# The last step of a top-k attention with a feed-forward layer behind it, and what follows it: exponentials, turns and dense pieces in another order

## The chip, the cores and the metric

The kernel runs on one core of one Trainium2 chip. The metric is the device time of one execution in microseconds (us); lower is better. Of the kernel before there are three runs without a profile and one execution with one.

## The reference

There are 8 batches of 8 heads, 576 tokens and 64 features. For each head the scores are scaled products of queries and keys; in each row only those that reach the 32nd largest are kept, a softmax is taken over them, and the result weighs the values. The heads side by side make 4608 tokens of 512 features, which go through a layer of width 2048 with a squared relu.

```python
scores = scale * np.matmul(q, k.transpose(0, 1, 3, 2))
kth = np.partition(scores, -32, axis=-1)[..., -32:-31]
scores = np.where(scores >= kth, scores, -1e9)
attn = np.exp(scores - np.max(scores, axis=-1, keepdims=True))
attn = attn / (np.sum(attn, axis=-1, keepdims=True) + 1e-09)
x = np.matmul(attn, v)          # then heads side by side: 4608 x 512
h = np.maximum(x @ w_in, 0.0)
out = h * h @ w_out
```

## The kernel before, in words

**Steps.** The attention is cut into U = 144 steps. A step holds 128 query rows of two heads (x = 0 and 1), each with 576 scores. The loop `for u in range(U)` (L688) writes out, by hand, the order in which each engine gets its instructions; `pin` keeps that order. The last four steps, U-4 to U-1, are the last 128 rows of the four head pairs of the last batch, so only when all four are placed is the last block of 128 tokens complete.

**What a step goes through.** `scores` makes the scores on PE (TensorE), and ACT (ScalarE) copies them to `s`. `topk` finds the 32nd largest on DVE (VectorE) by four rounds of MAX8 and three of MATCH_REPLACE8. For most steps `drop` (L373) then computes on POOL (GpSimd), from the negated ends `neg` (L361), what pushes the scores below the bound far down, and a DMA adds it to `s` (L382); `exps` (L386) takes the exponentials on ACT into `w_two`, one of three buffers a, b, c by u % 3; `turn` (L395) transposes `w_two` to `wT` with a DMA on SP's queue. For the last step, and for x = 1 of the one before it (`by_vector`, L355), it goes another way: `early_exps` (L364) takes the exponentials `e` of the unmasked scores on ACT, and `mask` (L388) multiplies them on DVE by the comparison with the bound.

**Turns.** The last two steps are turned by PE: `turn_by_tensor` (L399) makes four transposes for x = 0 and five for x = 1 into a PSUM bank (`sc_a` for U-2, `sc_b` for U-1) and copies each group to `wT`, by ACT for U-2 (L409), by DVE for U-1 (L411). The second group waits for the copy of the first.

**Products and placing.** `weigh` (L413; `products` calls it for both x) multiplies `wT` with the values into `av_ps`, or into `sc_a` for the last two steps, with the sum of the weights as a 65th column: ten matmuls a step. `invert` (L434) takes the reciprocal on DVE, and `place` (L444) scales on ACT into `x_tok`, two instructions a step. In the loop, step U-5 is placed in step U-1, which makes the last block but one complete.

**Blocks.** A complete block of 128 tokens is queued by `turn_x` (L683). For the last blocks of the last batch `x_unit` (L473) puts an entry into `moves`: four transposes of `x_tok` on PE (L489) and a copy `xT` on ACT (L490). Then `block` (L516) adds four *up pieces* to `ups` and, with the last of these, four *down pieces* to `downs`. An up piece is 16 matmuls with `w_in` (L533) into a bank `gen` (two of them) or, for every third once `tail` is set, `sc_b`; behind it come a relu on ACT (L538) and a square, on ACT (L544) or, once `late` is set, on DVE (L542). A down piece is 4 matmuls of 512 columns with `w_out` (L556) into the one bank `dn_ps`; the fourth is followed by a copy on ACT (L561) and a store on SP's queue (L563).

**Dense pieces as filling.** `piece` (L577) runs one piece, taken in turns from `ups` and `downs`. With `later` set it puts the relu and square of an up piece by in the list `behind`; no call before the change sets it. `dense` (L589) runs, for x = 1, one entry of `moves`, and one or two pieces. In the loop, `dense(u, 0)` and `dense(u, 1)` stand near the end of each step. In the last step they stand ahead of `early_exps(u)` and `exps(u - 1, 0)`.

**Behind the loop** (L735 to L771): the three masks, the turns of U-2, the last products, reciprocals and placings, with dense pieces between them; a reduction over flags on DVE (L753), its sum by a matmul (`count`, L761) and a copy (`bad`, L763), which says whether the general path below must run (it doesn't for this input); then the four ups and downs of the last block, each up piece beside a down piece of the block before, and four down pieces at the end.

**Order on the engines before**, from the loop's last step on, as built:

- PE: the products of U-5, two down pieces of the block that stands first, x_tok transposes, an up piece, the products of U-4, the turn of U-2 (sc_a), half the turn of U-1 (sc_b), a down piece, an up piece, the products of U-3, the other half of the turn of U-1, the products of U-2, an up piece, the products of U-1, an up piece, x_tok transposes, a down piece, the count, and then up and down pieces in turns.
- ACT: neg, x_tok (U-5), two exps of U-3 (w_two_a), xT, a relu, a square, neg, two e of U-1, an exp of U-2 (w_two_b), two copies of the turn of U-2, x_tok (U-4), and then relus, squares and x_tok.
- DVE: the last MAX8, three masks, a reciprocal, the first copy of the turn of U-1, a reciprocal, the second copy, two reciprocals, the reduction, and four squares as multiplications.

Of the kernel before, what the change touches and what calls it, by code (L numbers as in the profile page):

```python
# [23 lines left out]
def kernel(  # L24
# [20 lines left out]
    def pin(ins):  # L45
        tc.keep_in_program_order(ins)
        return ins
# [193 lines left out]
    U = len(steps)  # L241
# [113 lines left out]
    def by_vector(u, x):  # L355
        return u == U - 1 or (u == U - 2 and x == 1)

    def negate(u, ends):
        neg = small.tile([128, 2, 2], f32, name="neg", bufs=4)
        got = st[u]["ends"] if ends == 2 else st[u]["ends"][:, :, 0:1]  # L360
        pin(nc.scalar.activation(neg[:, :, 0:ends], got, AF.Copy, scale=-1.0))  # L361
        return neg

    def early_exps(u):  # L364
        d = st[u]
        neg = negate(u, 1)
        d["e"] = {}
        for x in range(2):
            if by_vector(u, x):
                e = d["e"][x] = scp.tile([128, S], bf16, name="e", bufs=3)  # L370
                pin(nc.scalar.activation(e[:, :], d["s"][:, x, :], AF.Exp, bias=neg[:, x, 0:1]))
# [12 lines left out]
    def exps(u, x):  # L384
        d = st[u]
        pin(nc.scalar.activation(w_two[u % 3][:, x, 0:S], d["s"][:, x, :], AF.Exp, bias=d["neg"][:, x, 0:1]))  # L386

    def mask(u, x):  # L388
        d = st[u]
        pin(nc.vector.scalar_tensor_tensor(out=w_two[u % 3][:, x, 0:S], in0=d["s"][:, x, :], scalar=d["m"][3][:, x, 7:8],  # L390
                                           in1=d["e"][x][:, :], op0=ALU.is_ge, op1=ALU.mult))
# [7 lines left out]
    def turn_by_tensor(u, x, by_scalar):  # L399
        if x == 0:  # L400
            st[u]["wT"] = scp.tile([128, 9, 128], bf16, name="wT", bufs=3)
            st[u]["tp"] = ps_sc.tile([128, 2, 1024], bf16, name="sc_" + "ab"[u - U + 2])
        flat = w_two[u % 3][:, :, :].rearrange("p x n -> p (x n)")
        tp = st[u]["tp"][:, x, 0:512 + 128 * x].rearrange("p (n r) -> p n r", r=128)
        for n in range(4 + x):
            pin(nc.tensor.transpose(tp[:, n, :], flat[:, (4 * x + n) * 128:(4 * x + n + 1) * 128], id_h[:, :]))
        to = st[u]["wT"][:, 4 * x:4 + 5 * x, :]
        if by_scalar:
            pin(nc.scalar.activation(to, tp, AF.Copy))  # L409
        else:  # L410
            pin(nc.vector.tensor_copy(to, tp))  # L411
# [15 lines left out]
    def sums(u):  # L427
        if u < U - 2:
            return av
        if not last_two:  # L430
            last_two["ps"] = ps_sc.tile([128, 2, 512], f32, name="sc_a")
        return last_two["ps"][:, u - (U - 2), 0:130].rearrange("p (x d) -> p x d", x=2)

    def invert(u):  # L434
        r = small.tile([128, 2, 1], f32, name="rsum", bufs=4)
        pin(nc.vector.reciprocal(r[:, :, :], sums(u)[:, :, 64:65]))  # L436
        st[u]["r"] = r
# [6 lines left out]
    def place(u):  # L444
        for x, (i, c, a) in enumerate(steps[u]):
            b, pr = pairs[i]
            o, r = sums(u)[:, x, :], st[u]["r"]
            if c < 4:
                if (b, c) not in x_tok:
                    x_tok[b, c] = ffp.tile([128, 512], bf16, name="x_tok", bufs=8)  # L450
                h = 2 * pr + a
                pin(nc.scalar.activation(x_tok[b, c][:, h * 64:(h + 1) * 64], o[:, 0:64], AF.Copy, scale=r[:, x, :]))
                left[b, c] = left.get((b, c), 8) - 1
                if left[b, c] == 0:
                    full.append((b, c))
            else:
                for g in range(2):
                    h, rows = 2 * pr + g, slice(64 * g, 64 * g + 64)
                    pin(nc.scalar.activation(x_rem[b % 2][rows, h * 64:(h + 1) * 64], o[rows, 0:64], AF.Copy, scale=r[rows, x, :]))
                left[b, 4] = left.get((b, 4), 4) - 1  # L460
                if left[b, 4] == 0:
                    soon_moves.append(lambda b=b: rem_unit(b))
        del st[u]


    moves, ups, downs = [], [], []
    soon_moves = []
    ripe = {}
    late, tail = [], []
# [99 lines left out]
    def idle_piece():  # L569
        hp = ps_one.tile([128, 512], f32, name="dn_ps")  # L570
        for kh in range(KH):
            pin(nc.tensor.matmul(out=hp[:, :], lhsT=id_h[:, :], rhs=fill[:, :], start=(kh == 0), stop=(kh == KH - 1)))

    turn_of = [0]
    behind = []

    def piece(later=False):  # L577
        turn_of[0] ^= 1
        for q_ in ((ups, downs), (downs, ups))[turn_of[0]]:
            if q_:  # L580
                rest = q_.pop(0)()
                if rest and later:
                    behind.append(rest)
                elif rest:
                    rest()
                return True
        return False

    def dense(u, x, later=False):  # L589
        for go in ripe.pop(u, ()):  # L590
            go()
        if moves and x == 1:
            rest = moves.pop(0)()
            if rest and later:
                behind.append(rest)
            elif rest:
                rest()
        if x == 1:
            moves.extend(soon_moves)
            soon_moves.clear()  # L600
        N = 2 if (u >= U - 26 and x == 0) or len(ups) + len(downs) > 24 else 1
        for n in range(N):
            if not piece(later and N == 1) and n == 0 and u < U:
                idle_piece()
# [65 lines left out]
    def ok(w):  # L670
        return 0 <= w < U

    def finish(w):
        if ok(w):
            invert(w)
            place(w)

    def products(w):
        if ok(w):
            for x in range(2):  # L680
                weigh(w, x)

    def turn_x(u):  # L683
        for b, c in full:
            x_unit(u, b, c)
        full.clear()

    for u in range(U):  # L688
        for x in range(2):
            if ok(u - 1) and not by_vector(u - 1, x):  # L690
                drop(u - 1, x)
        quads_of(u)
        topk(u, (0,))
        if ok(u - 4):
            invert(u - 4)
        if ok(u + 1):
            for i, c, a in steps[u + 1]:
                while coming <= i or (coming == i + 1 and soon):
                    prepare(u)
            scores(u + 1)  # L700
            both(u + 1)
        casts_next = bool(soon) and soon[0].__name__ == "values"
        for _ in range(0 if casts_next else 2 if u < 8 else 1):
            prepare(u)
        if ok(u - 4):
            place(u - 4)
        if ok(u - 2):
            exps(u - 2, 0)
            exps(u - 2, 1)
            turn(u - 2)  # L710
        fetch(10 if u < 8 else 3)
        if u >= Z:
            turn_x(u)
        topk(u, (1, 2))
        if ok(u + 1):
            pairs_of(u + 1)
            copy_far(u + 1)
            lesser(u + 1)
        topk(u, (3,))
        if casts_next:  # L720
            prepare(u)
        if by_vector(u, 1) and u < U - 1:
            early_exps(u)
        dense(u, 0)
        dense(u, 1)
        if u == U - 1:
            early_exps(u)
            exps(u - 1, 0)
        products(u - 3)
        turn_x(u)  # L730
        if w_casts and u >= 3:
            w_casts.pop(0)()
        if w_loads and u >= 1:
            w_loads.pop(0)()
    mask(U - 2, 1)  # L735
    mask(U - 1, 0)
    mask(U - 1, 1)
    turn_by_tensor(U - 2, 0, True)
    turn_by_tensor(U - 2, 1, True)
    finish(U - 4)  # L740
    turn_x(U)
    turn_by_tensor(U - 1, 0, False)
    dense(U, 0)
    products(U - 3)
    finish(U - 3)
    turn_by_tensor(U - 1, 1, False)
    products(U - 2)
    turn_x(U)
    dense(U, 1)
    products(U - 1)  # L750
    finish(U - 2)
    finish(U - 1)
    pin(nc.vector.tensor_reduce(worst[:, :], flags[:, :, :].rearrange("p f n -> p (f n)"), axis=mybir.AxisListType.X, op=ALU.max))  # L753
    pin(nc.vector.tensor_scalar(worst[:, :], worst[:, :], scalar1=0.0, scalar2=None, op0=ALU.is_gt))
    dense(U, 1)
    turn_x(U)
    late.append(True)
    tail.append(0)
    dense(U + 1, 1)
    count = ps_one.tile([128, 512], f32, name="gen", bufs=2)  # L760
    pin(nc.tensor.matmul(out=count[0:1, 0:1], lhsT=worst[:, :], rhs=ones[:, :], start=True, stop=True))  # L761
    bad = const.tile([1, 1], mybir.dt.int32, name="bad")
# [135 lines left out]
```

## Time and profile before

| | us |
|---|---|
| median of three runs | 940.19 |
| lowest, highest | 939.16, 942.92 |
| the profiled execution | 941.0 |
| its span, first to last instruction | 939.2 |
| DVE busy in it | 895.6 |
| ACT busy in it | 785.8 |
| POOL busy in it | 776.0 |
| PE busy in it | 685.7 |

The profile is of one execution. Engines are PE, PEld (PE's weight loads), DVE, ACT, POOL and SP. A timeline row gives the start in us from the span's start, the duration in us, the engine, the line of the kernel, the operation, the tile written and the tiles read, the shapes, and a count when several in a row are merged; in brackets stands how long the engine was idle before it and what released it. In merged rows of PE the ends are modelled, so the distance from one row's start to the next is the better price of a piece. A windows row gives a stretch, its length, the busy time of PE, PEld, DVE, ACT and POOL in it with the number of instructions, the clock that PE was granted as a share of full speed, the busy share of the DMA engines, and GB/s.

### The profile page before, as it was taken

The numbers are of one execution on the slowest core, as the hardware profiler recorded it, in microseconds if no ns is written. First come the engines' busy times: TensorE is split into PE (matmuls) and PEld (weight loads), VectorE is DVE, ScalarE is ACT, GpSimd is POOL, SyncE is SP. The second block draws the span as 40 slices with busy tenths as digits, with TensorE's granted clock in tenths as the row PEclk, the third lists the DMA queues.
The fourth block names the chain that finished last, engine by engine and source line by source line (L and its number), as shares of the span: only waits on it lengthen the run. The fifth ranks groups of instructions, "written<-read, shape, count | busy, mean of one in ns | idle before, by whom it ended". The sixth has DMA issues, their size and how long they took to land.

```text
span 939.2 us, 20939 instructions
## 1 busy us (share of the span) xinstructions
PE 685.7 (73%) x6176; PEld 434.4 (46%) x6176; DVE 895.6 (95%) x3633; ACT 785.8 (84%) x1780; POOL 776.0 (83%) x803
## 2 busy tenths in 40 slices
PE   6777676777777677776777777767777788787767
PEld 3333344444445444444454444444445455555444
DVE  6999999999999999999999999999999999999972
ACT  4677898889888988889888998888888888987884
POOL 7888889888888888888878889888898887897760
PEclk9998999899999999999989999999998998998989
DMA  5668866899998999889999999999999998886751
GB/s 140 135 156 167 176 133 131 180 196 200 200 199 182 200 205 202 188 191 194 203 189 179 191 207 200 207 184 194 189 205 193 199 211 175 167 180 135 147 115 38
DMA packets 329976, 166.29 MB, mean 177 GB/s; under 512 B 306560, under 2 KB 306560, under 8 KB 329856
## 3 DMA queue, kind: packets, MB, share of 16 engines
q1 hardware_dynamic: 311088, 92.62, 51.9%
q0 software_dynamic: 17568, 71.97, 33.8%
q8 instruction: 52, 0.85, 0.4%
q14 instruction: 68, 0.56, 0.2%
q10 hardware_dynamic: 1200, 0.30, 0.1%
HBM read 37.75 MB, written 9.44 MB: 50 GB/s over the span
## 4 chain that ended last, share of the span: by engine, by line
DVE 65%; issue 11%; ACT 9%; DMA 5%; PE 5%; POOL 2%; SPq 1%; POOLq 0%; ACTq 0%
DVE m L342 27%; DVE cat L346 17%; DVE sc_b L282 6%; DVE cat L292 5%; DVE cat L291 5%; DVE most L283 5%; DMA s<-gone_a 2%; PE sc_b L263 2%; ACT s L266 1%; ACT w_two_a L386 1%; DMA s<-gone_b 1%; PE gen L533 1%; PE dn_ps L556 1%; DVE rsum L436 1%; ACT rl L538 1%
## 5 line engine op out<-in xcount | busy, mean ns | idle before, releaser
L342 DVE MAX8 m<-cat 128x8 f32<-128x104 f32 (+3 forms) x1152 | 448.6, 433 | 0.0
L346 DVE MATCH_REPLACE8 cat<-m,cat 128x104 f32<-128x104 f32 (+2 forms) x864 | 272.1, 324 | 0.0
L307 POOL TENSOR_TENSOR cat<-s 128x576 int32<-128x576 int32 (+1 forms) x144 | 230.5, 1601 | 2.0 <-ACT s L266 2.0
L316 POOL TENSOR_TENSOR cat<-cat,most 128x576 int32<-128x576 int32 (+1 forms) x144 | 190.1, 1320 | 26.7 <-ACT most L298 14.9
L263 PE MATMUL sc_b<-qkT 64*128 64x288 f32 x512 | 109.8, 504 | 124.9 <-DVE cat L292 123.0
L533 PEld LDWEIGHTS <-w_in 128*128 128x128 bf16 x2304 | 152.4, 104 | 48.5 <-issue 27.8
L556 PE MATMUL dn_ps<-w_out,h 128*128 128x512 bf16 x576 | 165.2, 418 | 2.3 <-ACT wide L561 1.5
L533 PE MATMUL gen<-xT,w_in 128*128 128x128 bf16 x2032 | 145.3, 229 | 11.4 <-ACT xT L490 4.6
L266 ACT ACTIVATE s<-sc_b 128x576 f32<-128x576 f32 x144 | 93.3, 648 | 69.5 <-PE sc_b L263 64.4
L378 POOL TENSOR_SCALAR gone_b<-s,neg 128x576 uint8<-128x576 f32 x142 | 105.9, 746 | 30.4 <-ACT neg L361 21.1
L378 POOL TENSOR_SCALAR gone_a<-s,neg 128x576 uint8<-128x576 f32 x143 | 106.6, 746 | 28.2 <-ACT neg L361 18.6
L263 PE MATMUL sc_a<-qkT 64*128 64x288 f32 x512 | 100.6, 468 | 39.3 <-DVE most L283 28.9
L263 PEld LDWEIGHTS sc_b<-qkT 64*128 64x128 f32 x512 | 47.2, 206 | 176.2 <-issue 96.1
L266 ACT ACTIVATE s<-sc_a 128x576 f32<-128x576 f32 x144 | 91.3, 634 | 13.4 <-PE sc_a L263 12.4
L538 ACT ACTIVATE rl<-gen 128x512 f32<-128x512 f32 x143 | 85.7, 599 | 8.1 <-PE gen L533 7.2
L544 ACT ACTIVATE h<-rl 128x512 bf16<-128x512 f32 x140 | 88.2, 630 | 4.4
L422 PEld LDWEIGHTS <-wT 128*128 128x128 bf16 (+1 forms) x1600 | 59.7, 102 | 59.6 <-DMA wT<-w_two_a 24.7
L556 PEld LDWEIGHTS <-h 128*128 128x128 bf16 x576 | 54.6, 104 | 67.3 <-issue 30.7
L386 ACT ACTIVATE w_two_a<-s,neg 128x576 bf16<-128x576 f32 x96 | 69.3, 777 | 5.3 <-DMA s<-gone_a 4.3
L386 ACT ACTIVATE w_two_b<-s,neg 128x576 bf16<-128x576 f32 x95 | 68.7, 779 | 5.5 <-DMA s<-gone_b 3.9
L282 DVE TENSOR_TENSOR sc_b<-sc_a,s 128x288 f32<-128x288 f32 x144 | 66.3, 460 | 5.1 <-ACT s L266 5.0
L382 POOL DMA_DIRECT2D s<-gone_b x61 | 54.1, 888 | 20.2 <-DVE m L342 8.3
(165 smaller groups left out, 1198.4 us busy)
## 6 DMA issues: line engine op xcount, KB each, us to landing
s<-gone_a POOLq DMA_DIRECT2D x61, 576.0 KB, 4.9
s<-gone_b POOLq DMA_DIRECT2D x61, 576.0 KB, 4.7
v_raw<-in_v_dram SPq DMA_DIRECT2D x64, 128.0 KB, 3.2
out_dram<-wide SPq DMA_DIRECT2D x32, 256.0 KB, 4.2
k_raw<-in_k_dram SPq DMA_DIRECT2D x63, 128.0 KB, 3.3
q_raw<-in_q_dram SPq DMA_DIRECT2D x63, 128.0 KB, 3.2
wide<-in_moe_w_in_dram SPq DMA_DIRECT2D x8, 512.0 KB, 4.4
wide<-in_moe_w_out_dram SPq DMA_DIRECT2D x8, 512.0 KB, 4.0
```

Source lines behind the costliest of these rows:

```text
L263: pin(nc.tensor.matmul(out=ps[j][:, x, 0:HALF], lhsT=lhsT, rhs=rhs, start=True, stop=True))
L266: pin(nc.scalar.activation(s[:, :, j * HALF:(j + 1) * HALF], ps[j][:, :, 0:HALF], AF.Copy))
L282: pin(tt(far, one[:, :, QUAR:HALF], two[:, :, QUAR:HALF], op=ALU.max))
L307: pin(tt(less, s[:, :, 0:wide].bitcast(i32), s[:, :, HALF:HALF + wide].bitcast(i32), op=ALU.add))
L316: pin(tt(less, less, d["most"][:, 0:n_h, :, :].bitcast(i32).rearrange("p h x n -> p x h n"), op=ALU.subtract))
L342: pin(nc.vector.max(out=m[r][:, x, :], in_=part(r, x)))
L346: pin(nc.vector.match_replace(out=part(r, x), in_to_replace=m[r][:, x, :], in_values=part(r, x), imm_value=NEG))
L378: pin(nc.gpsimd.tensor_scalar(byte[:, x, :, 1], s[:, x, :], scalar1=d["neg"][:, x, 1:2], scalar2=-HUGE, op0=ALU.add, op1=ALU.mult))
L386: pin(nc.scalar.activation(w_two[u % 3][:, x, 0:S], d["s"][:, x, :], AF.Exp, bias=d["neg"][:, x, 0:1]))
L533: pin(nc.tensor.matmul(out=hp[:, n * n_rows:(n + 1) * n_rows], lhsT=w_in[:, kh, (f0 + n) * 128:(f0 + n + 1) * 128], rhs=xt(kh), start=(kh ...
L538: pin(nc.scalar.activation(rl[:, :], hp, AF.Relu))
L556: pin(nc.tensor.matmul(out=op[:, :], lhsT=held["h2"][:, f, c * 128:(c + 1) * 128], rhs=w_out[:, f, :], start=(f == 0), stop=(f == NF - 1)))
```

## The change

All of it lies in the last step of the loop and behind the loop.

1. In the last step, as soon as U-5 is placed, the complete block is queued and its x_tok transposes and xT copy are made at once, ahead of the exponentials of U-3.
2. `early_exps` of the last step and the exponential of U-2 come ahead of the dense pieces, and there are two pieces instead of three, with their relu and square put by. A third such piece stands between the masks and the turn.
3. The four halves of the two turns follow each other with no dense piece between; behind them come the products of U-2, U-3 and U-1, and the three reciprocals.
4. `late` is set there, so that all squares of the two blocks left are DVE's. Then the relus that were put by run (`flush`), then the three placings.
5. A down piece, the x_tok transposes of the last block, the reduction over the flags, an up and a down piece follow, then the count and the rest as before.

As built, the number of instructions changes on ACT only by the four squares that go to DVE. The order from the last step on is now:

- PE: the products of U-5, x_tok transposes, an up piece, a down piece, the products of U-4, an up piece, the whole turn of U-2, the whole turn of U-1, the products of U-2, U-3 and U-1, a down piece, x_tok transposes, an up piece, a down piece, the count, an up piece, and then down and up pieces in turns, with four down pieces at the end.
- ACT: neg, x_tok (U-5), xT, two exps of U-3 (w_two_a), neg, two e of U-1, an exp of U-2 (w_two_b), two copies of the turn of U-2, x_tok (U-4), two relus, x_tok (U-2, U-3, U-1), xT, and then relus and evictions.
- DVE: the last MAX8, three masks, a reciprocal, both copies of the turn of U-1, three reciprocals, two multiplications, the reduction, and six multiplications.

```diff
             place(u - 4)
+        if u == U - 1:
+            turn_x(u)
+            while moves:
+                moves.pop(0)()
         if ok(u - 2):
...
-        if by_vector(u, 1) and u < U - 1:
+        if by_vector(u, 1):
             early_exps(u)
-        dense(u, 0)
-        dense(u, 1)
-        if u == U - 1:
-            early_exps(u)
+        if u < U - 1:
+            dense(u, 0)
+            dense(u, 1)
+        else:
             exps(u - 1, 0)
+            piece(True)
+            piece(True)
         products(u - 3)
...
     mask(U - 1, 1)
+    def flush():
+        while behind:
+            behind.pop(0)()
+
+    assert not ripe and not moves and not soon_moves
+    piece(True)
     turn_by_tensor(U - 2, 0, True)
     turn_by_tensor(U - 2, 1, True)
     finish(U - 4)
-    turn_x(U)
     turn_by_tensor(U - 1, 0, False)
-    dense(U, 0)
-    products(U - 3)
-    finish(U - 3)
     turn_by_tensor(U - 1, 1, False)
     products(U - 2)
-    turn_x(U)
-    dense(U, 1)
+    products(U - 3)
     products(U - 1)
-    finish(U - 2)
-    finish(U - 1)
+    for w in (U - 2, U - 3, U - 1):
+        invert(w)
+    late.append(True)
+    flush()
+    for w in (U - 2, U - 3, U - 1):
+        place(w)
+    tail.append(0)
+    piece()
+    turn_x(U)
     pin(nc.vector.tensor_reduce(worst[:, :], flags ...))
     pin(nc.vector.tensor_scalar(worst[:, :], worst[:, :], ...))
-    dense(U, 1)
-    turn_x(U)
-    late.append(True)
-    tail.append(0)
-    dense(U + 1, 1)
+    while moves:
+        moves.pop(0)()
+    piece()
+    piece()
     count = ps_one.tile([128, 512], f32, name="gen", bufs=2)
```

More of the change, by code (lines that the diff above doesn't have):

```diff
@@ L740 @@
     finish(U - 4)
-    turn_x(U)
     turn_by_tensor(U - 1, 0, False)
-    dense(U, 0)
-    products(U - 3)
-    finish(U - 3)
     turn_by_tensor(U - 1, 1, False)
     products(U - 2)
+    products(U - 3)
+    products(U - 1)
+    for w in (U - 2, U - 3, U - 1):
[6 more added lines that the diff above has]
+    piece()
     turn_x(U)
-    dense(U, 1)
-    products(U - 1)
-    finish(U - 2)
-    finish(U - 1)
     pin(nc.vector.tensor_reduce(worst[:, :], flags[:, :, :].rearrange("p f n -> p (f n)"), axis=mybir.AxisListType.X, op=ALU.max))
     pin(nc.vector.tensor_scalar(worst[:, :], worst[:, :], scalar1=0.0, scalar2=None, op0=ALU.is_gt))
-    dense(U, 1)
-    turn_x(U)
-    late.append(True)
-    tail.append(0)
-    dense(U + 1, 1)
+    while moves:
+        moves.pop(0)()
+    piece()
+    piece()
     count = ps_one.tile([128, 512], f32, name="gen", bufs=2)
```

## The prediction

> **What bounds the kernel now.** I read the page's busy shares first, then the chain that ended last, then the timeline engine by engine from 899 us on, then the windows.
>
> ```profile
> span 939.2 us, 20939 instructions
> ```
>
> DVE has the highest share and sets the pace: in the windows below it is busy 3.42 of 3.42 us and 3.41 of 3.41 up to 907.17, and it has no gap until its last MAX8. The change leaves every DVE instruction up to there alone. So 906.20 + 1.41 = 907.5 us stays, and the change can only act on the 31.7 us behind it.
>
> ```profile
> 906.20 1.41 DVE L342 MAX8 m<-cat 128x8 f32<-128x576 f32 x2
> 911.08 1.54 DVE L390 SCALAR_TENSOR_TENSOR w_two_c<-s,m,e 128x576 bf16<-128x576 f32 x2 [2.75 <-ACT e L371]
> ...
> 904.34 0.50 ACT L452 ACTIVATE x_tok<-av_ps,rsum 128x64 bf16<-128x64 f32 x2
> 905.09 1.44 ACT L386 ACTIVATE w_two_a<-s,neg 128x576 bf16<-128x576 f32 x2 [0.26 <-DMA s<-gone_b]
> 906.43 0.57 ACT L490 ACTIVATE xT<-gen 128x512 bf16<-128x512 bf16 x1
> ...
> 909.51 0.63 ACT L544 ACTIVATE h<-rl 128x512 bf16<-128x512 f32 x1
> 910.05 0.19 ACT L361 ACTIVATE neg<-m 128x2 f32<-128x2 f32 x1
> 910.27 1.44 ACT L371 ACTIVATE e<-s,neg 128x576 bf16<-128x576 f32 x2
> 911.62 0.76 ACT L386 ACTIVATE w_two_b<-s,neg 128x576 bf16<-128x576 f32 x1
> ```
>
> At 907.5 the selection is done, but the last step's exponentials (e, L371) stand on ACT behind a relu and a square, which wait for a matmul piece. So the masks (L390) sit 2.75 us, and the turn of step U-2 starts only behind w_two_b, at 912.4. From there PE does everything:
>
> ```profile
> 907.06 1.79 PE L533 MATMUL gen<-xT,w_in 128*128 128x128 bf16 x16 [1.94 <-ACT xT L490]
> 908.64 0.76 PE L422 MATMUL av_ps<-vau_e,wT 128*128 128x65 bf16 x10
> 912.43 0.61 PE L406 MATMUL sc_a<-id_h,w_two_b 128*128 128x128 bf16 x4 [3.03 <-ACT w_two_b L386]
> 913.73 0.69 PE L406 MATMUL sc_a<-id_h,w_two_b 128*128 128x128 bf16 x5 [0.69 <-ACT wT L409]
> 914.64 1.91 PE L556 MATMUL dn_ps<-w_out,h 128*128 128x512 bf16 x4
> 916.35 1.57 PE L533 MATMUL gen<-xT,w_in 128*128 128x128 bf16 x16
> ...
> 918.06 0.45 PE L406 MATMUL sc_b<-id_h,w_two_c 128*128 128x128 bf16 x5
> 918.34 0.47 PE L422 MATMUL sc_a<-vau_a,wT 128*128 128x65 bf16 x10
> ...
> 922.22 0.23 PE L489 MATMUL gen<-id_h,x_tok 128*128 128x128 bf16 x1 [0.53 <-ACT x_tok L452]
> 922.28 1.03 PE L556 MATMUL dn_ps<-w_out,h 128*128 128x512 bf16 x4
> ...
> 923.85 1.05 PE L533 MATMUL gen<-xT,w_in 128*128 128x128 bf16 x16 [0.42 <-ACT bad L763]
> 924.74 1.03 PE L556 MATMUL dn_ps<-w_out,h 128*128 128x512 bf16 x4
> 925.60 1.06 PE L533 MATMUL gen<-xT,w_in 128*128 128x128 bf16 x16
> ...
> 930.01 3.62 PE L556 MATMUL dn_ps<-w_out,h 128*128 128x512 bf16 x16
> ```
>
> From start to start, an up piece (L533 x16) takes 0.89 us and a down piece (L556 x4) 0.86 at full clock; PE ends at 930.01 + 3.62 = 933.63. Early in this stretch the same pieces take twice that. The windows, cut every 3.41 us, show why:
>
> ```profile
> 900.34:903.76 3.42, 2.05 (x18) 0.90 (x18) 3.42 (x13) 3.33 (x8) 3.34 (x3) 1.00 0.77 205
> 903.76:907.17 3.41, 1.02 (x9) 0.49 (x8) 3.41 (x16) 2.99 (x7) 2.42 (x3) 1.00 0.60 111
> 907.17:910.58 3.41, 2.23 (x26) 2.06 (x24) 1.16 (x2) 1.63 (x4) 1.45 (x3) 0.50 0.45 87
> 910.58:914.00 3.42, 0.88 (x8) 0.72 (x8) 1.63 (x3) 2.39 (x4) 0.00 (x0) 0.50 0.00 0
> 914.00:917.41 3.41, 3.41 (x22) 2.29 (x21) 0.42 (x1) 1.71 (x4) 0.00 (x0) 0.50 0.00 0
> 917.41:920.82 3.41, 3.41 (x77) 3.41 (x75) 0.83 (x3) 2.68 (x6) 0.00 (x0) 1.00 0.36 82
> ...
> 163.06:166.48 3.42, 3.01 (x29) 2.61 (x29) 3.42 (x11) 3.04 (x8) 2.95 (x5) 0.50 0.80 171
> 166.48:169.89 3.41, 3.19 (x11) 1.07 (x10) 3.41 (x19) 3.17 (x9) 3.16 (x4) 0.50 1.08 264
> ```
>
> The second number is PE's busy time, the third from the end its clock. The clock is 1.00 or 0.50 for a whole window and changes at the edges only. A warm window with 2.05 us busy is followed by a warm one, one with 1.02 by a cold one; of the cold ones, 3.01 is followed by a cold one and 3.41 by a warm one. So the line down lies between 1.02 and 2.05, the line up between 3.01 and 3.41. PE is cold from 907.17 to 917.41: just where the turns stand.
>
> **The change part by part.**
>
> *Early exponentials.* The x_tok transposes now come right behind place(U-5): x_tok ends at 904.84, the last transpose (0.23) at 905.15, and the xT copy (0.5 before the next can start) stands ahead of w_two_a, which starts at 905.7 instead of 905.09: 0.6 later. Behind it, by the rows' starts: w_two_a 1.34, neg 0.2, e 1.35, w_two_b 0.76 end at 909.4 instead of 912.4. Gone from between are the wait for the up piece (907.06 to 908.85), its relu and its square. The masks follow e (908.7) at 0.77 us each and end by 910.3 instead of 912.6. The DMA that turns w_two_a starts 0.6 later on SP; its reader, the products of U-3, comes near 914, so this costs nothing; without that cover 0.6.
>
> *Dense pieces of the last step.* Ahead of the turn PE now has an up piece, a down piece, the products of U-4 and a second up piece, all behind the xT copy, from 905.8. Two down pieces leave the place where they kept PE busy; one now follows the first up piece, the other goes past the turns, and so does the one at 914.64:
>
> ```profile
> 901.36 1.03 PE L556 MATMUL dn_ps<-w_out,h 128*128 128x512 bf16 x4
> 903.24 1.04 PE L556 MATMUL dn_ps<-w_out,h 128*128 128x512 bf16 x4 [0.85 <-ACT h L544]
> ```
>
> Window 900.34 to 903.76 loses 1.03 + 0.52 of its 2.05 us and gains three transposes of at most 0.4, which leaves 0.9: PE goes cold at 903.76, a window earlier. Cold, an up piece takes 1.7 (908.64 - 907.06, of which 0.11 was warm), a down piece 1.7 (916.35 - 914.64), ten products 0.6 to 0.76. So up 905.8 to 907.5, down to 909.2, products to 909.8, and the second up piece would end at 911.5. But window 907.17 to 910.58 is now full, PE is warm from 910.58, and the piece ends at 911.1. The turn starts there, 1.7 us after its data but 1.3 before the turn of before.
>
> *Turns without dense pieces.* Warm, from 911.1: four transposes 0.43, copy 0.66 with its hand-over, five transposes (0.28 until the next starts), four of U-1 0.43, DVE's copy 0.48, five 0.48, and the second copy:
>
> ```profile
> 914.88 0.42 DVE L411 COPY wT<-sc_b 128x512 bf16<-128x512 bf16 x1 [2.17 <-PE sc_b L406]
> 918.54 0.49 DVE L411 COPY wT<-sc_b 128x640 bf16<-128x640 bf16 x1
> ...
> 921.53 1.33 DVE L753 TENSOR_REDUCE worst<-flags 128x1 f32<-128x1152 f32 x1
> 925.57 0.69 DVE L542 TENSOR_TENSOR h<-rl 128x512 bf16<-128x512 f32 x1 [2.52 <-ACT rl L538]
> ...
> 921.64 0.52 ACT L452 ACTIVATE x_tok<-sc_a,rsum 128x64 bf16<-128x64 f32 x2 [0.24 <-DVE rsum L436]
> 922.05 0.60 ACT L538 ACTIVATE rl<-gen 128x512 f32<-128x512 f32 x1
> ```
>
> That is 914.4 (before: 919.0). Products of U-2 and U-3 lie in the wait for it; those of U-1 end at 914.9. Window 910.58 to 914.00 holds about 2.3 us of work (0.5 of the up piece, its 0.15 us drain, 1.15 and 0.5 of turns and products), above the 2.05 of the row that stayed warm: PE stays warm. With drains counted otherwise it is 1.9 to 2.6, so this is close, and its other side is rival B.
>
> *Relus put by.* The two relus (0.60 each) run on ACT behind the U-2 copy, from 913.8 to 915.0, before the reciprocals of the products exist, so they cost nothing; without that cover 1.2. Their squares become DVE multiplications of 0.69 behind the reciprocals, 915.3 to 916.6; PE reads the first at 919.3.
>
> *Placing.* Reciprocals from 914.9, the first result at 915.1; three pairs of x_tok on ACT, 0.42 + 0.42 + 0.50: 916.45; the last transpose starts at 916.5 instead of 922.22. One down piece fills PE meanwhile.
>
> *What is left for PE.* Here the change gives back. Before, four ups and eight downs stood behind that transpose, from 922.28 on; now six ups and nine downs do, 6 x 0.89 + 9 x 0.86 = 13.1, with the count 0.1, and 0.17 for the last matmul's drain. From 916.5 that ends at 929.9. PE is the bound here: the last xT copy is done at 917.3 and its reader comes at 920.1; the flag for the count (1.33 and a short second instruction on DVE, behind the two multiplications) is ready at about 918.0, and PE asks for it at 918.3. Should it be late, PE waits as long.
>
> *Sum.* 933.63 - 929.9 = 3.7 us. Behind PE's end nothing changes: the eviction, the store and the end, 5.6 us. The span becomes 935.5; the profiled execution, 941.0 us, becomes 937.3. It was 0.8 above the median of 940.19, so the median's version is 936.5; I forecast 936.9, between the two.
>
> *Two rules against rows.* Whether the turn counts as work for the clock, and what a gap costs, decides more than any instruction. The window 914.00 to 917.41 began with 0.64 us of transposes and ended in full clock, while a window with 3.01 us busy did not: without the transposes it had 2.77. The Trainium skill, TensorE: Matmul & The Clock Gate, Part 4 (PE-mode transpose), says that transposes do not count as PE work for the gate. By that rule window 910.58 to 914.00 would count about 1.0 us, and the clock would go as in rival B. Window 903.76 to 907.17 had 1.02 us of work and still cost the clock. The same page's Part 1 says that the clock drops after at least one idle window, and no window here would be wholly idle; by that rule PE stays warm, which is rival A, and the row speaks against it.
>
> **The rivals.**
>
> *A. PE is warm as the turn starts.* The edges can lie elsewhere against the work in another execution. If they fall 1.7 to 2.7 us later, which is a third of their 3.41 us, the window that ends near 909 is full, the second up piece runs at full clock and the turn starts at 910.2, 0.9 earlier: 936.4. If PE never goes cold, the turn starts with its data at 909.4, all later steps move up 1.7, and the gain is 5.4: 935.6, or 934.8 against the median. Against it: the 0.9 us of work in the window up to 903.76, less than in the 1.02 row.
>
> *B. PE goes cold in the turn.* If transposes don't count, 914.00 to 917.41 runs at half clock, where PE has about 3 us of work: 1.5 us lost, 938.8; a further half window lost gives 939.6. The warm-up row above speaks against it.
>
> *C. PE doesn't warm before the last block (slower than before).* The place is window 907.17 to 910.58. By the 3.01 row it warms PE only with a hole of less than 0.4 us in it; a late wT of U-4 or a late xT decides. Past that point the second up piece ends at 911.8, the turn goes at half clock as in the rows of before, its waits leave holes in the next two windows as well, and the last transpose stands 6.6 us on (5.6 as worked out, 1.0 for slower transposes and products), at 918.4. Then window 917.41 to 920.82 has a hole too, and PE is cold to 924.24. Of its 13.2 us of work it does 2.9 by then, and ends at 934.7: 1.1 slower, 942.1. Against it: the pieces ahead of the turn wait for nothing but xT and a wT that was issued a step earlier.
>
> *D. Nothing comes of it*, because the tail hangs on stores or code loading: 941. PE's unbroken rows from 923.85 to 933.63 speak against it.
>
> **How the numbers follow.** Forecast (a gain of 2.9 to 4.7): 0.55. A: 0.25. B: 0.10. C: 0.05. D: 0.05. About 0.5%, 4.7 us, is what a measurement of this kernel can tell from no change; the forecast's 3.7 lies below that, A's 5.4 above. Faster by over 0.5%: most of A and a little of the forecast, where the median's scatter carries it over, 0.27; slower by as much: C and a late flag together, 0.04; within: 0.69. The range takes in A against the median (934.8, less 0.4 for the median's own scatter) and B with the further half window (939.6): 934.4 to 939.6. It leaves out C, D and the edges of A and B.
>
> **What would show it.** Right: w_two_b ends near 909.4; the masks follow without the 2.75 us wait; the turn begins at 911 with transposes of full-clock length; the last x_tok transpose stands near 916.5; PE runs from there without a gap for 13.3 us. Wrong: cold windows between 911 and 917 (B, C), PE idle behind 916.5 for the count or for relus, or a turn that starts before 910 (A).

## The result, and the profile after

The changed kernel takes 938.74 us (median of 22 runs, 935.01 to 942.98), the kernel before, run beside it, 942.02 (22 runs, 938.59 to 948.4). The ratio is 0.9966, with a 95% interval of 0.9952 to 0.9980: 3.2 us faster, 1.9 to 4.5. The prediction's 936.9 against 940.19 is 0.9965. In absolute terms 938.74 lies 1.8 above the forecast and inside its range, 934.4 to 939.6; the kernel before stands 1.8 above its first median of 940.19 as well.

The two profiled executions have spans of 939.2 and 936.5 us. But they don't reach the change at the same time: the first mask (L390, right behind the last MAX8) starts at 907.53 before and at 908.90 after, though no instruction up to the last step was moved. In the profiles below that point lies between 902.12 and 917.39. So I measure from there. Two rows of the windows view follow, first before and then after, from the first mask to PE's end; the second number is PE's busy time, the third from the end its mean clock:

```profile
907.53:933.63 26.10, 20.98 (x225) 15.01 (x222) 8.02 (x16) 14.14 (x30) 1.45 (x3) 0.81 0.14 34
```

```profile
908.90:930.87 21.97, 20.14 (x223) 13.22 (x220) 10.57 (x20) 11.34 (x25) 2.35 (x3) 0.96 0.17 40
```

I call this length the *tail*: 26.10 us before, 21.97 after, 4.13 less, at a mean clock of 0.96 instead of 0.81. Each tail, here and below, is that of one execution. Behind PE's end both need 5.6 us for the last eviction and store. The timeline of after, DVE, ACT and then PE:

```profile
907.57 1.43 DVE L342 MAX8 m<-cat 128x8 f32<-128x576 f32 x2
908.90 0.82 DVE L390 SCALAR_TENSOR_TENSOR w_two_b<-s,m,e 128x576 bf16<-128x576 f32 x1
909.62 1.78 DVE L390 SCALAR_TENSOR_TENSOR w_two_c<-s,m,e 128x576 bf16<-128x576 f32 x2
...
914.54 0.49 DVE L411 COPY wT<-sc_b 128x640 bf16<-128x640 bf16 x1 [0.53 <-PE sc_b L406]
...
907.12 1.43 ACT L386 ACTIVATE w_two_a<-s,neg 128x576 bf16<-128x576 f32 x2
908.45 0.19 ACT L361 ACTIVATE neg<-m 128x2 f32<-128x2 f32 x1
908.68 1.44 ACT L371 ACTIVATE e<-s,neg 128x576 bf16<-128x576 f32 x2
910.02 0.76 ACT L386 ACTIVATE w_two_b<-s,neg 128x576 bf16<-128x576 f32 x1
...
914.36 1.10 ACT L538 ACTIVATE rl<-gen 128x512 f32<-128x512 f32 x2
915.88 0.52 ACT L452 ACTIVATE x_tok<-sc_a,rsum 128x64 bf16<-128x64 f32 x2 [0.43 <-DVE rsum L436]
...
907.27 1.86 PE L533 MATMUL gen<-xT,w_in 128*128 128x128 bf16 x16 [0.69 <-ACT xT L490]
908.93 1.85 PE L556 MATMUL dn_ps<-w_out,h 128*128 128x512 bf16 x4
910.62 0.47 PE L422 MATMUL av_ps<-vau_e,wT 128*128 128x65 bf16 x10
910.92 1.06 PE L533 MATMUL gen<-xT,w_in 128*128 128x128 bf16 x16
911.82 0.39 PE L406 MATMUL sc_a<-id_h,w_two_b 128*128 128x128 bf16 x4
912.89 0.44 PE L406 MATMUL sc_a<-id_h,w_two_b 128*128 128x128 bf16 x5 [0.69 <-ACT wT L409]
...
914.95 0.50 PE L422 MATMUL sc_a<-vau_b,wT 128*128 128x65 bf16 x10
...
927.25 3.62 PE L556 MATMUL dn_ps<-w_out,h 128*128 128x512 bf16 x16
```

The masks no longer wait: the 2.75 us that stood behind e is gone. w_two_b ends at 910.78, 1.88 behind the first mask (before: 4.85). The turn starts at 911.82, at 2.92 (before: 4.90), right behind the second up piece, and its transposes have the length of the full clock (0.39 instead of 0.61). The two relus that were put by run in a row at 914.36, ahead of the first x_tok, which waits for the reciprocals anyway. The windows of after, cut at the same edges as those of before, which happen to fit this execution too:

```profile
900.34:903.76 3.42, 2.06 (x27) 1.23 (x25) 3.42 (x11) 3.39 (x9) 3.05 (x4) 1.00 0.85 179
903.76:907.17 3.41, 0.56 (x4) 0.26 (x4) 3.41 (x20) 3.03 (x9) 2.85 (x4) 1.00 1.01 220
907.17:910.58 3.41, 3.31 (x20) 2.26 (x20) 3.41 (x7) 3.38 (x7) 2.44 (x3) 0.50 0.26 52
910.58:914.00 3.42, 2.29 (x40) 2.01 (x39) 1.31 (x4) 1.44 (x4) 0.85 (x2) 1.00 0.20 37
914.00:917.41 3.41, 2.72 (x45) 1.86 (x45) 2.43 (x8) 2.79 (x11) 0.00 (x0) 1.00 0.02 5
```

And the end of the chain of waits of after, in order of time (start, length, what):

```profile
915.88 1.35 ACT x_tok L452 x6
917.23 0.04 issue
917.28 0.23 PE gen L489
917.51 0.89 PE gen L533 x16
918.40 0.86 PE dn_ps L556 x4
919.26 0.12 PE gen L774 x2
919.38 1.00 PE gen L533 x16
```

From the last x_tok transpose, 917.28, to PE's end, 927.25 + 3.62 = 930.87, PE has nothing but its pieces and the count.

In the windows there is one cold one instead of three. It is the one that the dense pieces fill (3.31 us), and the clock is back before the turn starts. The turn's own window holds 2.29 us and stays warm.

### The profile page after: what moved, and what is told of

Read it like the earlier page. It is cut to its first block, busy times and chain, and to the rows that moved or that the text cites. A ratio compares the mean times of both kernels' runs of the same rounds, so it can differ in the third digit from the quotient of the medians.

```text
span 936.5 us, 20941 instructions
## 1 busy us (share of the span) xinstructions
PE 678.4 (72%) x6176; PEld 429.6 (46%) x6176; DVE 898.1 (96%) x3637; ACT 784.2 (84%) x1776; POOL 778.8 (83%) x803
## 4 chain that ended last, share of the span: by engine, by line
DVE 70%; issue 10%; PE 8%; ACT 6%; DMA 5%; POOL 1%; SPq 0%; ACTq 0%; POOLq 0%
DVE m L342 29%; DVE cat L346 18%; DVE sc_b L282 6%; DVE cat L292 5%; DVE cat L291 5%; DVE most L283 5%; PE dn_ps L556 2%; PE sc_b L263 2%; PE gen L533 1%; PE sc_a L263 1%; DMA wT<-w_two_a 1%; DMA wT<-w_two_c 1%; ACT s L266 1%; DVE rsum L436 1%; DMA v_raw<-in_v_dram 1%
## 5 line engine op out<-in xcount | busy, mean ns | idle before, releaser
L342 DVE MAX8 m<-cat 128x8 f32<-128x104 f32 (+3 forms) x1152 | 461.2, 455 | 0.0
L346 DVE MATCH_REPLACE8 cat<-m,cat 128x104 f32<-128x104 f32 (+2 forms) x864 | 281.1, 346 | 0.0
L533 PEld LDWEIGHTS <-w_in 128*128 128x128 bf16 x2304 | 149.6, 103 | 49.5 <-issue 28.5
L533 PE MATMUL gen<-xT,w_in 128*128 128x128 bf16 x2016 | 140.7, 226 | 12.7 <-ACT rl L538 6.0
L544 ACT ACTIVATE h<-rl 128x512 bf16<-128x512 f32 x136 | 85.8, 631 | 4.3
L346 DVE MATCH_VALUE_LOAD cat<-m,cat 128x8 f32 x864 | 89.1, 103 | 0.0
L282 DVE TENSOR_TENSOR sc_b<-sc_a,s 128x288 f32<-128x288 f32 x144 | 69.6, 484 | 6.1 <-ACT s L266 6.0
L291 DVE TENSOR_TENSOR cat<-sc_b,most 128x288 f32<-128x288 f32 x144 | 67.3, 467 | 5.2 <-ACT most L298 5.0
```

Source lines behind the costliest of these rows:

```text
L282: pin(tt(far, one[:, :, QUAR:HALF], two[:, :, QUAR:HALF], op=ALU.max))
L291: pin(tt(cat[:, :, 0:QUAR], far, near, op=ALU.max))
L342: pin(nc.vector.max(out=m[r][:, x, :], in_=part(r, x)))
L346: pin(nc.vector.match_replace(out=part(r, x), in_to_replace=m[r][:, x, :], in_values=part(r, x), imm_value=NEG))
L533: pin(nc.tensor.matmul(out=hp[:, n * n_rows:(n + 1) * n_rows], lhsT=w_in[:, kh, (f0 + n) * 128:(f0 + n + 1) * 128], rhs=xt(kh), start=(kh ...
L544: pin(nc.scalar.activation(h2, flat, AF.Square))
```

## The experiments

Three things could carry the gain: the earlier exponentials, the shorter chain of the turns, and PE's clock. The theory was that all three are needed and that PE is the bound behind the turn, that is, that work added to or taken from PE there moves the end by as much. The rivals were that one of them does it alone. Each run's tail row (from the first mask to PE's end) stands below; the expectations count to the end of the span, about 5.6 us more.

**e1_exps_first.** One part alone, in the kernel before:

```diff
-        if by_vector(u, 1) and u < U - 1:
+        if by_vector(u, 1):
             early_exps(u)
+        if u == U - 1:
+            exps(u - 1, 0)
         dense(u, 0)
         dense(u, 1)
-        if u == U - 1:
-            early_exps(u)
-            exps(u - 1, 0)
```

> The kernel before, with one part of the change alone: in the last step the early exponentials and the exponential of U-2 stand ahead of the dense pieces. Measured from the start of the first mask (L390, right behind the last MAX8) to the end of the span, which is 31.7 us before and 27.6 after. Theory (the exponentials alone free the masks, but PE still has its cold up piece ahead of the turn, and the relu and square still stand between the copies of the turn): the turn starts about 0.7 us earlier, 30.8 to 31.2. Rival (the exponentials are the whole change): 27.6 to 28.5.

Measured: ratio 1.0006 (0.9976 to 1.0036), 30.9 us to the end of the span. The tail row and PE's rows ahead of the turn:

```profile
908.77:933.97 25.20, 20.87 (x225) 15.39 (x227) 8.25 (x16) 13.54 (x29) 2.34 (x3) 0.82 0.14 35
```

```profile
910.53 1.86 PE L533 MATMUL gen<-xT,w_in 128*128 128x128 bf16 x16 [4.18 <-ACT xT L490]
912.18 0.76 PE L422 MATMUL av_ps<-vau_e,wT 128*128 128x65 bf16 x10
912.75 0.62 PE L406 MATMUL sc_a<-id_h,w_two_b 128*128 128x128 bf16 x4
```

The exponentials come earlier, but now xT stands behind them, PE idles 4.18 us for it, and the cold up piece still stands ahead of the turn. As the theory said: the order of the exponentials alone takes 0.9 us off the tail. Part of that can be the edges of the windows: PE's clock comes back 8.8 us behind the first mask here and 9.9 before.

**e2_relus_at_once and e8_warm_relus_at_once.** Putting by undone, in the changed kernel and in e3_keep_warm (below):

```diff
-            piece(True)
-            piece(True)
+            piece()
+            piece()
...
-    piece(True)
+    piece()
     turn_by_tensor(U - 2, 0, True)
```

> The changed kernel, but the relus and squares of the two up pieces ahead of the turn run at once on ACT. Theory: relu and square of the second up piece stand ahead of the first copy of the turn, which comes 1.0 us later, and everything behind it as well, since PE is the bound: 28.6 us from the first mask to the end of the span. Rival (PE has slack there, so putting by is worth nothing): 27.6 as after.

> As e3_keep_warm, but with the relus and squares of the two up pieces ahead of the turn at once on ACT (as in e2_relus_at_once, without its cold clock). Theory: two relus and two squares stand between w_two_b and the first copy of the turn, which comes 1.9 us later: 28.8 us from the first mask to the end of the span. Rival (they fit in ACT's gaps): 27.0.

Measured: e2 0.9980 (0.9951 to 1.0009), 30.5 us to the end of the span; e8 0.9973 (0.9948 to 0.9998), 30.2 us. Both misses, on the slow side. Of e2 the tail row, the turn's window and the next one stand below, of e8 the tail row and PE's second half of the turn of U-2:

```profile
908.53:933.22 24.69, 22.11 (x219) 15.14 (x220) 9.44 (x18) 12.52 (x27) 2.36 (x3) 0.86 0.15 36
...
912.06:915.47 3.41, 1.28 (x20) 1.04 (x19) 0.42 (x1) 2.42 (x5) 0.00 (x0) 1.00 0.00 0
915.47:918.88 3.41, 3.19 (x38) 2.58 (x38) 1.53 (x5) 1.04 (x6) 0.00 (x0) 0.50 0.02 5
```

```profile
907.81:932.04 24.23, 20.57 (x215) 14.42 (x216) 9.35 (x18) 12.52 (x27) 2.35 (x3) 0.86 0.15 37
```

```profile
912.57 0.69 PE L406 MATMUL sc_a<-id_h,w_two_b 128*128 128x128 bf16 x5 [2.37 <-ACT wT L409]
```

In e8 the second half of the turn waits 2.37 us instead of 0.69 for the first copy, which stands behind two relus and two squares: 1.7 us, near the 1.9 expected. What was left out is what that hole does to the clock: the turn's window holds little (1.28 us in e2) and the clock falls in the turn. e8 against e3_keep_warm is 24.23 against 20.94, 3.3 us. But e11_keep_warm_again (below), where the relus are put by, loses the clock in the turn as well, and against its 21.88 the difference is 2.35. So putting by is worth 2.4 to 3.3 us here: 1.7 for the delay, and the rest goes with the clock, which falls earlier and for longer in e8 (two windows from 911.78) than in e11 (one).

**e3_keep_warm, and again as e11_keep_warm_again.** PE kept busy where it waits for x_tok of U-5:

```diff
+    def warm(n):
+        hp = ps_sc.tile([128, 2, 512], f32, name="sc_a")
+        for k in range(n):
+            pin(nc.tensor.matmul(out=hp[:, 0, :], lhsT=id_h[:, :], rhs=fill[:, :], start=(k == 0), stop=(k == n - 1)))
...
         if u == U - 1:
+            warm(12)
             turn_x(u)
```

> The changed kernel with 12 more matmuls (128x512, into the free bank sc_a, whose result is never read) where PE waits for x_tok of U-5. Theory (the clock falls because that window is less than half busy): the clock stays 1.00, the two up pieces and the down piece take 0.9 each, the turn starts with w_two_b instead of 1.0 us behind it, 26.6 us from the first mask to the end of the span. Rival (the clock doesn't matter for this stretch, or the added matmuls delay the x_tok transposes): 27.6 or more.

> The kernel of e3_keep_warm once more. Theory: 1.0 us below the changed kernel run beside it, ratio to the kernel before 0.994 to 0.997, 26.9 us from the first mask to the end of the span wherever the edges fall. Rival (its first run was a lucky phase): no difference from the changed kernel.

Measured: e3 0.9938 (0.9904 to 0.9972), e11 0.9941 (0.9914 to 0.9968); to the end of the span 26.9 and 27.6 us, where 26.6 and 26.9 were expected. The tail row of e3, then that of e11 with its turn's window and the next:

```profile
917.39:938.33 20.94, 18.50 (x215) 12.60 (x215) 10.55 (x20) 11.26 (x25) 2.36 (x3) 1.00 0.18 42
```

```profile
908.29:930.17 21.88, 19.76 (x215) 13.68 (x215) 10.58 (x20) 11.31 (x25) 2.36 (x3) 0.92 0.17 40
...
909.13:912.54 3.41, 1.74 (x26) 1.33 (x24) 2.18 (x4) 2.39 (x5) 1.71 (x3) 1.00 0.45 86
912.54:915.96 3.42, 3.20 (x38) 2.59 (x39) 1.67 (x6) 2.08 (x8) 0.00 (x0) 0.50 0.02 5
```

In both, the turn starts right behind w_two_b, 1.0 us earlier than after. In e3 the clock stays at 1.00 and all of it arrives at the end: 1.03 us less than after. In e11 the edges cut the turn so that a window holds 1.74 us, the clock falls inside the turn, and 0.94 is lost again: the tail of 21.88 is no shorter than that of the changed kernel beside it (after_again, 21.89). "Wherever the edges fall" was wrong, and the rival of e11 was right in part: the fill keeps the clock up to the turn, and whether it falls in the turn is a matter of the edges. By time the two stand 0.28% and 0.18% below the changed kernel, within the intervals.

**e4_turns_first.** The three dense pieces ahead of the turn go behind the products:

```diff
             exps(u - 1, 0)
-            piece(True)
-            piece(True)
...
-    piece(True)
     turn_by_tensor(U - 2, 0, True)
...
     products(U - 1)
+    for n in range(3):
+        piece(True)
     for w in (U - 2, U - 3, U - 1):
         invert(w)
     late.append(True)
-    flush()
     for w in (U - 2, U - 3, U - 1):
         place(w)
+    flush()
```

> The changed kernel with the three dense pieces ahead of the turn put behind the products, and their relus behind the placings. Theory (those pieces warm PE for the turn): the turn starts 1.0 us earlier but at half clock, and PE is cold until some 10 us behind the first mask or a window longer: 30.1 or 31.8 us from the first mask to the end of the span. Rival (the pieces only delay the turn): 26.6 to 27.6.

Measured: 0.9970 (0.9943 to 0.9998); 30.6 us to the end of the span. The tail row and two of its windows:

```profile
906.37:931.40 25.03, 21.73 (x223) 15.85 (x226) 10.63 (x20) 11.31 (x25) 2.34 (x3) 0.83 0.15 35
...
904.47:907.88 3.41, 0.73 (x10) 0.57 (x10) 3.41 (x7) 3.38 (x7) 2.35 (x3) 0.50 0.24 49
907.88:911.30 3.42, 1.90 (x16) 1.58 (x17) 1.47 (x4) 1.94 (x5) 0.99 (x2) 0.50 0.22 41
```

The turn starts 1.1 us earlier than after, and the tail is 3.1 us longer: the whole turn goes at half clock. In these two executions the pieces ahead of the turn pay for themselves. The times don't show it (a ratio of 0.9970 against 0.9966); the two intervals leave room for about 3 us at most.

**e5_before_warm.** The kernel before, with `warm` put in at two places and nothing else:

```diff
         dense(u, 0)
+        if u == U - 1:
+            warm(8)
         dense(u, 1)
...
         products(u - 3)
+        if u == U - 1:
+            warm(14)
         turn_x(u)
```

> The kernel before, with 8 more matmuls (128x512, result never read) in its last step ahead of the x_tok transposes and 14 more ahead of the turn of U-2, so that PE is kept busy where it waited. Theory (of the 4.1 us between the two kernels a large part is the clock): the up piece ahead of the exponentials takes 0.9, the turn starts 0.9 earlier and runs at full clock, and the down and up piece inside it take half: about 28.8 us from the first mask to the end of the span, against 31.7 before and 27.6 after. Rival (the order of the work is what counts, not the clock): 31 or more.

Measured: 0.9979 (0.9953 to 1.0006), 28.9 us to the end of the span, as expected. The tail row:

```profile
909.94:933.29 23.35, 20.85 (x233) 13.96 (x233) 8.02 (x16) 14.13 (x30) 1.44 (x3) 1.00 0.16 38
```

22 matmuls whose result nobody reads take 2.75 us off the old order's tail; the ratio of the times says 2.0, and its interval just includes no change. With e3 this divides the gain between the profiled executions: at full clock the old order takes 23.35 and the new one 20.94, so the order is worth 2.41; the old one lost 2.75 to the clock and the new one, as profiled, 1.03, so the clock is worth 1.72. Together the 4.13.

**e7_warm_transposes.** Do transposes count as work for the clock? e3's 12 matmuls replaced:

```diff
-        hp = ps_sc.tile([128, 2, 512], f32, name="sc_a")
+        hp = ps_sc.tile([128, 2, 1024], bf16, name="sc_a")
         for k in range(n):
-            pin(nc.tensor.matmul(out=hp[:, 0, :], lhsT=id_h[:, :], rhs=fill[:, :], start=(k == 0), stop=(k == n - 1)))
+            pin(nc.tensor.transpose(hp[:, 0, 0:128], fill[:, 0:128], id_h[:, :]))
...
-            warm(12)
+            warm(46)
```

> As e3_keep_warm, with 46 transposes of 128x128 in place of the 12 matmuls of 128x512, which take PE the same 2.6 us. Theory (transposes count as work for the clock): the clock stays 1.00 and the turn starts with w_two_b, 26.9 us from the first mask to the end of the span. Rival (the Trainium skill, TensorE: Matmul & The Clock Gate, Part 4: transposes don't count): the clock falls to 0.50 ahead of the up pieces as in the changed kernel, 27.6 or more.

Measured: 0.9947 (0.9919 to 0.9976), 26.8 us to the end of the span. The tail row, the stretch in which PE does nothing but transposes, and one window of the clock twice: with all of PE's work, and with that of the up piece (L533) alone:

```profile
902.12:923.04 20.92, 18.48 (x214) 12.60 (x215) 10.55 (x20) 11.25 (x25) 2.35 (x3) 1.00 0.21 42
...
896.20:900.40 4.20, 2.91 (x50) 2.62 (x47) 4.20 (x21) 3.81 (x10) 3.66 (x4) 1.00 0.98 214
```

```profile
897.48:900.90 3.42, 2.11 (x36) 1.82 (x33) 3.42 (x21) 3.07 (x8) 2.96 (x3) 1.00 0.84 175
```

```profile
897.48:900.90 3.42, 0.48 (x9) 0.58 (x10) 1.00 0.84 175
```

The clock stays at 1.00. The edges of this execution follow from the clock's fall at 928.20, behind PE's end: nine windows of 3.413 us earlier lies 897.48. The window from there holds 2.11 us of work, of which only the 0.48 of the up piece are not transposes, and the clock is still 1.00 in the next one. In the fourteen profiles here (without their first 15 us) every warm window with less than 1.44 us of work was followed by a cold one. So here transposes count, against the rule of the Trainium skill (TensorE: Matmul & The Clock Gate, Part 4, PE-mode transpose) that the prediction weighed.

**e10_more_work.** e3_keep_warm with `warm(4)`, a down piece's work, behind the last x_tok transposes.

> As e3_keep_warm, with 4 more matmuls of 128x512 (a down piece's work, result never read) behind the last x_tok transposes. Theory (PE is the bound from there to the end): 0.9 us more, 27.8 us from the first mask to the end of the span. Rival (PE has slack there): 26.9.

Measured: 0.9954 (0.9932 to 0.9976), 28.2 us to the end of the span. The tail row:

```profile
909.42:932.15 22.73, 20.64 (x219) 14.07 (x219) 10.56 (x20) 11.25 (x25) 2.35 (x3) 0.92 0.16 39
```

The fair partner is e11, which lost its clock at nearly the same place (4.2 us behind the first mask in both): 22.73 against 21.88, 0.85 for a piece of 0.86. PE has no slack there.

**e6_holes, and mended as e9_holes_mended.** If PE is the bound, the holes of the turn are worth filling. e9's edit of e3_keep_warm, in short:

```diff
     turn_by_tensor(U - 2, 0, True)
+    piece(True)
+    finish(U - 4)
     turn_by_tensor(U - 2, 1, True)
-    finish(U - 4)
     turn_by_tensor(U - 1, 0, False)
+    products(U - 3)
+    finish(U - 3)
     turn_by_tensor(U - 1, 1, False)
     products(U - 2)
-    products(U - 3)
     products(U - 1)
...
```

The reduction over the flags also goes ahead of the multiplications, and a down piece fills the wait for the last x_tok. In e9 both relus stand ahead of the placings, and the order of the last pieces is written out. e6 has `finish(U - 4)` behind the turn of U-2, one relu behind the placings, and the last pieces in turns.

> The changed kernel with PE kept busy as in e3_keep_warm, and the holes of the turns used: a down piece between the two halves of the turn of U-2, the products of U-3 between the halves of the turn of U-1, U-3 placed there already, a down piece while the last x_tok is made, one relu put behind the placings, the flag reduced ahead of the multiplications. Theory (PE is the bound, so each hole that is filled and the 0.4 of placing U-3 come off the end): 25.1 us from the first mask to the end of the span, against 26.9 of e3_keep_warm. Rival (the pieces in the turns make the chain longer by what they take from its end): 26.5 or more.

> As e6_holes, mended where it waited: U-4 is placed between the two copies of the turn of U-2, both relus stand ahead of the placings, and the last pieces are ordered so that no down piece waits for the eviction of dn_ps. Theory (PE is the bound; a down piece and the placing of U-3 come off): the last x_tok transpose 7.0 us behind the first mask and PE's end 19.6, 25.3 to 25.5 us from the first mask to the end of the span. Rival (the chain of the turns takes back what the holes give): 26.5 or more.

Measured: e6 0.9966 (0.9939 to 0.9993), 27.4 us to the end of the span; e9 0.9924 (0.9902 to 0.9947), 25.2. e6 missed by 2.3 us; its tail row, and the two waits that took 1.67 of them:

```profile
906.64:928.31 21.67, 18.75 (x214) 12.77 (x215) 10.65 (x20) 11.06 (x25) 2.35 (x3) 1.00 0.17 41
```

```profile
911.29 0.46 PE L422 MATMUL av_ps<-vau_f,wT 128*128 128x65 bf16 x10 [0.98 <-ACT x_tok L452]
...
924.70 3.61 PE L556 MATMUL dn_ps<-w_out,h 128*128 128x512 bf16 x16 [0.69 <-ACT wide L561]
```

The products of U-3 need `av_ps` free, and U-4 was placed only behind the second copy; and with two down pieces gone from the end, two others stood against each other over `dn_ps`. e9 removes both, and its tail is the shortest, 1.26 us below that of e3:

```profile
904.83:924.51 19.68, 18.45 (x214) 12.76 (x215) 10.62 (x20) 11.21 (x25) 2.36 (x3) 1.00 0.19 45
```

PE is busy for 18.45 of 19.68 us. Beside the changed kernel on the same chip (after_again) it takes 932.78 against 935.19 us (medians of 6 and 10 runs).

**after_again.** The changed kernel once more.

> The changed kernel once more, beside the two others on the same chip: a ratio to the kernel before of 0.995 to 0.998, and 27.6 us from the first mask to the end of the span if the edges of the clock fall as before, up to 0.5 more or 1.0 less if not.

Measured: 0.9959 (0.9936 to 0.9982), 27.2 us to the end of the span; its tail is 21.89 us at 0.96, as in the first profile (21.97).

## Why the prediction was right, step by step

The order of the work did what the prediction said, and PE is the bound that it named. But it took the edges of the windows from the profile of before, and in the profiled execution of after they fell elsewhere against the work; that this made the tail shorter and not longer is luck. Times are counted from the first mask, which the prediction put at 907.5.

- *Exponentials*: w_two_b was to end at 1.9, and ended at 1.88. The masks follow without a wait. Shown.
- *Dense pieces and clock*: PE was to go cold at 903.76, because window 900.34 to 903.76 would hold 0.9 us. It held 2.06, since the work stood 1.4 us later against the edges than I had assumed; the next one, with 0.56, cost the clock instead. So there is one cold window, where the prediction had two. The mechanism held: the window full of pieces warms PE just ahead of the turn. The turn was to start at 3.6, and started at 2.92: the largest error of the sum, 0.65 us on the good side.
- *Turn*: from its start to the last x_tok transpose 5.4 us; the chain of waits gives 917.28 - 911.82 = 5.46.
- *What is left for PE*: 13.4 us from there; 930.87 - 917.28 = 13.59, of which 0.1 is the up piece behind the count (1.00 in the chain instead of 0.89); no row shows what held it. e10 shows that PE is the bound.
- *Sum*: 3.7 us less; the tail is 4.13 shorter, 0.4 more (0.65 from the earlier turn, less 0.06 and 0.19 from the two steps behind it), and the medians give 3.2 (1.9 to 4.5). So the forecast, "within 0.5%", holds.
- *Turns as work for the clock*: e7 shows that transposes count. The prediction's own argument, a window that would have held 2.77 us without them and warmed PE, was too weak: in e4 a window with 2.67 us (389.06 to 392.47) was followed by a warm one too, so there is no firm line between the 3.01 and 3.41 that the prediction read from two windows. *Gaps*: a window need not be idle; 0.56 and 1.74 us of work cost the clock.
- *Rival A*, its first case, is what the profiled execution shows. Against the work the edges lie 2.04 us later than before (1.37 earlier, in steps of 3.41), inside the 1.7 to 2.7 that this case asked for: the window ahead of the turn is full, and the second up piece runs at full clock (0.90 from start to start). The turn came 0.65 earlier than forecast, where the case said 0.9. Its second case, PE never cold, is e3: 1.03 us against my 1.7, since the turn had started 0.65 earlier already.
- *Rival B* was right in its place and wrong in its reason: the clock does fall in the turn in some executions (e2, e8, e10, e11; neither of the two of the changed kernel itself), not because transposes don't count but because of where the edges lie. It costs 0.94 (e11 against e3), I had 1.5, and my 1.9 to 2.6 us for the turn's window was too narrow, as I had fixed the edges: e11 has 1.74.
- *Rival C* needs the pieces gone: e4, where the tail is 25.03, longer than after by 3.1 but not longer than before.
- *Rival D* falls: PE's end moved by the 4.13 us, and the 5.6 us behind it stayed.

What stays open is how often each position of the edges comes (both profiles of the changed kernel have nearly the same), and so how much of the medians' scatter is the clock and how much is the time lost ahead of the last step.

## What to carry to other kernels

At the end of a kernel, where one engine's last result starts a chain over PE, count two things from one point: what stands ahead of the chain on each engine, and what PE has left behind it. Here the dense pieces belonged ahead of the chain, where they also bring the clock up, and into its holes only if neither they nor their evictions hold a buffer or an engine that the chain needs. And when executions differ in front of the change, compare stretches that start at the same instruction, not spans.

## What was not expected of the hardware

PE's clock is 1.00 or 0.50 in windows of 3.41 us whose edges keep their distance through a whole execution (in e7 the clock changes at 856.52 and at 928.20, 21 windows apart), but not their place from one to the next: the clock falls at 907.17 before and after, at 905.23 in e2, at 904.47 in e4, and in e2 it changes again whole windows later (912.06, 915.47). A window with 1.74 us of work lost the clock and one with 2.05 kept it, but PE's busy time doesn't settle it near that line: in the kernel before a window with 1.73 (879.86 to 883.28) kept the clock, and in e11 one with 2.00 (830.62 to 834.04) lost it. In the old order 22 matmuls without any use were worth 2.75 us.
